# Routing and expert stage of a fused retention and mixture kernel: key digits made together, 16-bit index tables, routing work moved to GpSimd, and new costs in the planner's table

## The chip, the cores and the metric

One core of one Trainium2 chip. The metric is the device time of the whole kernel in microseconds (us), the median of three timed runs. A profiled execution with a trace of every instruction lies beside them. The core's engines are TensorE (PE, with its weight loads as PEld), VectorE (DVE), ScalarE (ACT) and GpSimd (POOL). Each takes its instructions in order, and the queue of SyncE (SP) issues most of the DMAs.

## The reference

```python
# attention (retention) over B=4, H=8, S=768, D=64, then:
x = attn_out as 3072 tokens x 512
h = x @ w_in; g = s * max(h, 0)**2 + b; x = g @ w_out          # 512 -> 2048 -> 512
# second stage: 8 experts, 384 tokens each
logits = x @ w_gate                                            # 3072 x 8
order = np.argsort(-logits.flatten())
for idx in order:                                              # greedy: best pair first
    tok, e = idx // 8, idx % 8
    if assigned[tok] >= 0 or counts[e] >= 384: continue
    assigned[tok] = e; counts[e] += 1
for e in range(8):
    out[assigned == e] = max(x[assigned == e] @ w1[e], 0) @ w2[e]   # 512 -> 1024 -> 512
```

The greedy assignment is sequential by nature. The kernel does it in eight rounds: each round finds the expert that fills up first and the logit at which it does, closes it, and goes on with the tokens that are left.

## The kernel before, in words

The kernel runs four parts one after the other: the retention and first dense stage (`retention`, `moes`), the middle blocks (`moe1`), the last block with the logits (`h_pair`, `x_last`), and the part that the change touches, from line 886 on: the search for each expert's tokens, and the experts' two matrix products.

Matrix products are done in two halves per operand (high part and remainder, `h` and `l`, `gh` and `gl`), as three matmuls each.

**The last part.** For each round i the work is:

- `begin(i)` (L924): over the open experts each token's best logit `m`, the expert `mx` that it belongs to, a one-hot `Eh` (L947) and a sixteenfold copy `EH` of it, in four pieces of 128x768 on ScalarE (L954); then the logit as an integer key (L960, L961) and its first digit (L969, L974, L980).
- `search(i)` (L1002): the threshold is found digit by digit, in six steps. In each the PE counts with 24 matmuls (L988) how many tokens of each expert reach each digit value, DVE picks the largest value at which some expert is full (L1034 to L1040) and compares the next digit with it (L969 for the digit, L1027, L980). At the end come the state updates (L1081 to L1084) and the slot numbers (L1073 to L1092).
- `index(i)` (L1102): from the slots two one-hot tables `oa` and `ob` and a payload `pay` are built on DVE (L1117 to L1126), 24 matmuls (L1131) and one more (L1139, two entries in the trace) put the token numbers in place, and DVE makes `idx` (L1142, L1145), the 384 rows of the round's expert.
- `fetch(i)` (L1149): three indirect DMAs by GpSimd (L1156) gather these rows from `x2d` in DRAM into the tile `big`, 128 rows each. The PE transposes them (L1170, twelve of 128x128 in groups), ACT and DVE split them into `gh` and `gl` (L1164, L1166).
- The expert's products in `mains` (L1333): `eh_unit` (L1295, 96 matmuls of 384 columns an expert) and `ey_unit` (L1315, 72 of 512 columns). Its rows are scattered to the output by GpSimd (L1323).
- Weights: `e_load` by SP (L1259), `e_high` on ACT (L1267), `e_low` on DVE (L1277).

In round 0 the last 128 rows of `x2d` are still being made (`x_last`, L854) while the search runs, and their contribution comes through a one-hot matmul (`one_hot` L1208, `last_row`, L1183). The first gather waits until the row blocks 21 to 23 are written to `x2d` (L861 on ACT, L863 the DMA).

**What sets the order.** Each engine runs its program in order, so the order of the instructions decides who waits. It is made at build time by a small planner (`Plan`, L76). Each strand of work is a generator that yields records `(engine, nanoseconds, needs, gives, latency, keep)`. The planner holds a clock for each engine and the time of each named result, and always emits the record that can begin first. `keep` is added to the needs of a PE record (600 ns for the search and the transposes) so that the PE gets other work in the meantime. What the planner takes as a gather's price is in `fetch`: 1000 ns of GpSimd for each of the three, and 2600 ns from there to the data (`LAT`, L118):

```python
LAT = {"PE": 190.0, "ACT": 50.0, "DVE": 50.0, "POOL": 2600.0, "Q": 2500.0}
yield op("POOL", 1000, ("idx", i), "w3" if i else "x2d", gives=("xg", i, t))
yield pe(340, *(("xg", i, t) for t in range(GT)), need, gives=("T", i, kc), keep=KEEP)
```

A record that is a lambda is a condition in the planner's order, and no instruction.

Of the kernel before, what the change touches and what calls it, by code (L numbers as in the profile page):

```python
# [20 lines left out]
F32 = mybir.dt.float32  # L21
# [11 lines left out]
FAR = 1.0e6  # L33
# [111 lines left out]
def kernel(  # L145
# [653 lines left out]
    POOL.tensor_copy(jt, iota[:, 0:NT + 1, None].to_broadcast([128, NT + 1, 2]))  # L799
    closed = rt.tile([128, E], F32, name="closed")  # L800
# [120 lines left out]
    SH = [32 - sum(BW[:s + 1]) for s in range(len(BW))]  # L921

    def begin(i):
# [32 lines left out]
        plan.add(repeat(), 100)  # L956
        yield dve(720)
# [4 lines left out]
        d = start_of(digit(key, 0))  # L962
        yield dve(950, gives=("cmp", i, 0))
        d, cmp = compare(d, 1, NT)
        ME[i] = (key, mx, EH.rearrange("p c r e -> p c (r e)"), d, cmp)
# [36 lines left out]
    def search(i):  # L1002
# [11 lines left out]
        else:  # L1014


            key, mx, EH, d, cmp = ME.pop(i)
            for s, w in enumerate(BW):

                n = (1 << w) - 1 if s + 1 < len(BW) else NL  # L1020
                yield pe(810 if n == NT else 620, ("cmp", i, s), ("EH", i, NC - 6), gives=("cnt", i, s), keep=KEEP)
                cnt = count(EH, cmp, n)
                yield dve(360)
# [70 lines left out]
        if not last:  # L1094
            yield dve(400)
            ta = rt.tile([128, NC], F32, name="ta")
            DVE.scalar_tensor_tensor(ta, s1[:, NC:], float(CAP), stb[:, NC:2 * NC], op0=OP.is_le, op1=OP.mult)
            DVE.tensor_tensor(Uf, Uf, ta, op=OP.subtract)
            if i + 2 < E:
                yield from begin(i + 1)  # L1100

    def index(i):  # L1102

        yield dve(630, ("s1", i))
        s1 = SLOT.pop(i)
        sl = rt.tile([128, NC], I32, name="sl")
        DVE.scalar_tensor_tensor(sl, s1[:, 0:NC], -1.0, s1[:, NC:], op0=OP.add, op1=OP.add)
# [4 lines left out]
        lowp = rt.tile([128, NC], I32, name="lowp")  # L1112
        DVE.tensor_scalar(lowp, sl, UP - 1, None, op0=OP.bitwise_and)
        DVE.tensor_scalar(sl, sl, UP.bit_length() - 1, None, op0=OP.arith_shift_right)
        yield dve(760)
        ob = rt.tile([128, NC, WP], F16, name="ob")
        DVE.tensor_tensor(ob, sl[:, :, None].to_broadcast([128, NC, WP]),  # L1117
                          iota[:, None, 0:WP].to_broadcast([128, NC, WP]), op=OP.is_equal)
        yield dve(560)
        oa = rt.tile([128, NC, UP], F16, name="oa")  # L1120
        DVE.tensor_tensor(oa, lowp[:, :, None].to_broadcast([128, NC, UP]),
                          iota[:, None, 0:UP].to_broadcast([128, NC, UP]), op=OP.is_equal)
        yield dve(880, gives=("pay", i))
        pay = rt.tile([128, NC, 2, UP], F16, name="pay")
        DVE.tensor_scalar(pay[:, :, 1, :], oa, pcv[:, 1, 0:1], None, op0=OP.mult)
        DVE.tensor_tensor(pay[:, :, 0, :], oa, pcv[:, 0, :, None].to_broadcast([128, NC, UP]), op=OP.mult)  # L1126
# [21 lines left out]
    def fetch(i):  # L1148
# [50 lines left out]
    def one_hot():  # L1199

        yield dve(600, "sl0", ("x", NF2 - 1, 3, None), gives="oneh")
# [5 lines left out]
        for k in range(GT):  # L1207
            DVE.tensor_scalar(o[:, k * 128:(k + 1) * 128].rearrange("p (u v) -> p u v", u=UP), at, float(k * 128), SL0,  # L1208
# [199 lines left out]
    plan.add(e_low(), 200)  # L1408
# [87 lines left out]
```

## Time and profile before

| | |
|---|---|
| median of 3 timed runs | 1021.79 us (1015.84 to 1022.62) |
| the profiled execution, its own time | 1010.83 us |
| its span, first to last instruction | 1009.0 us |
| mean granted TensorE clock | 0.992 |
| PE busy | 971.9 us (96%) |
| DVE, ACT, POOL busy | 708.6, 472.0, 68.9 us |

How to read it: PE is busy nearly all the time, so shares of the whole span show little. A row of the timeline gives the time for which its engine stood still before it in brackets, with what ended it. The rows of a timeline merge equal instructions that follow each other ("x24"), with the time from the first start to the last end. Ends of matmuls are modelled, so the distance from one matmul's start to the next one's is its price when the PE is not waiting.

### The profile page before, as it was taken

The numbers are of one execution on the slowest core, as the hardware profiler recorded it, in microseconds if no ns is written. First come the engines' busy times: TensorE is split into PE (matmuls) and PEld (weight loads), VectorE is DVE, ScalarE is ACT, GpSimd is POOL, SyncE is SP. The second block draws the span as 40 slices with busy tenths as digits, with TensorE's granted clock in tenths as the row PEclk, the third lists the DMA queues.
The fourth block names the chain that finished last, engine by engine and source line by source line (L and its number), as shares of the span: only waits on it lengthen the run. The fifth ranks groups of instructions, "written<-read, shape, count | busy, mean of one in ns | idle before, by whom it ended". The sixth has DMA issues, their size and how long they took to land.

```text
span 1009.0 us, 18595 instructions
## 1 busy us (share of the span) xinstructions
PE 971.9 (96%) x7296; PEld 854.8 (85%) x7296; DVE 708.6 (70%) x1778; ACT 472.0 (47%) x953; POOL 68.9 (7%) x90
## 2 busy tenths in 40 slices
PE   7899999999999999999999999989999998999897
PEld 6899998889998999989989777777878787788796
DVE  5898983688887788788772623677878777788510
ACT  6766766444344444444443552343453543345411
POOL 2000000000000000000000100011120311113111
PEclk8999999999999999999999999999999999999999
DMA  9233442532212021212130100334243433427400
GB/s 344 88 129 139 151 146 95 160 99 83 89 32 91 26 70 57 64 63 64 53 110 14 47 1 2 115 127 157 85 176 128 147 117 114 157 85 243 175 32 32
DMA packets 32952, 103.58 MB, mean 103 GB/s; under 512 B 4512, under 2 KB 4896, under 8 KB 32864
## 3 DMA queue, kind: packets, MB, share of 16 engines
q1 hardware_dynamic: 28080, 88.15, 26.5%
q0 software_dynamic: 3920, 12.89, 3.6%
q10 hardware_dynamic: 864, 1.35, 0.4%
q8 instruction: 57, 0.93, 0.4%
q14 instruction: 31, 0.25, 0.1%
HBM read 89.53 MB, written 12.85 MB: 101 GB/s over the span
## 4 chain that ended last, share of the span: by engine, by line
PE 86%; DMA 6%; issue 4%; POOL 2%; DVE 1%; ACT 0%; POOLq 0%; SPq 0%; ACTq 0%; DVEq 0%
PE b L434 27%; PE b L467 22%; PE b L1295 10%; PE b L1315 9%; DMA big<-x2d,idx 4%; PE b L854 4%; PE b L341 3%; PE b L354 3%; PE b L988 2%; PE b L368 2%; POOL big L1156 1%; PE b L1170 1%; PE b L362 1%; PE b L837 1%; DMA x2d<-tmp 1%
## 5 line engine op out<-in xcount | busy, mean ns | idle before, releaser
L490 DVE SCALAR_TENSOR_TENSOR scr<-tmp,wg 128x512 bf16<-128x512 f32 x288 | 198.2, 688 | 9.0 <-ACT tmp L477 3.7
L434 PE MATMUL b<-xh,h 128*128 128x256 f32 (+1 forms) x640 | 189.0, 295 | 1.5 <-ACT xh L659 1.5
L434 PE MATMUL b<-xl,h 128*128 128x256 f32 (+1 forms) x640 | 188.2, 294 | 0.3 <-DVE xl L661 0.3
L434 PE MATMUL b<-xh,l 128*128 128x256 f32 (+1 forms) x640 | 188.2, 294 | 0.0
L434 PEld LDWEIGHTS b<-xh,h 128*128 128x128 f32 x640 | 122.3, 191 | 11.0 <-ACT xh L659 1.7
L434 PEld LDWEIGHTS b<-xl,h 128*128 128x128 f32 x640 | 122.3, 191 | 7.9 <-DVE xl L661 0.5
L467 PE MATMUL b<-h,rh 128*128 128x512 f32 x320 | 128.7, 402 | 0.0
L467 PE MATMUL b<-l,rh 128*128 128x512 f32 x320 | 126.1, 394 | 0.0
L467 PE MATMUL b<-h,rl 128*128 128x512 f32 x320 | 124.8, 390 | 0.0
L434 PEld LDWEIGHTS b<-xh,l 128*128 128x128 f32 x640 | 122.2, 191 | 2.8
L441 ACT ACTIVATE r<-b 128x256 f32<-128x256 f32 x112 | 43.0, 384 | 166.1 <-PE b L434 158.7
L1295 PE MATMUL b<-gh,h 128*128 128x384 f32 x256 | 89.6, 350 | 0.0
L1300 ACT ACTIVATE hh<-b 128x384 fp32r<-128x384 f32 x64 | 31.4, 491 | 123.5 <-PE b L1295 122.8
L1295 PE MATMUL b<-gl,h 128*128 128x384 f32 x256 | 86.2, 337 | 0.2 <-DVE gl L1166 0.2
L1295 PE MATMUL b<-gh,l 128*128 128x384 f32 x256 | 86.3, 337 | 0.0
L1267 ACT ACTIVATE h<-eraw 128x1024 fp32r<-128x1024 f32 x64 | 66.8, 1056 | 27.1 <-DMA eraw<-in_w_dram 26.5
L1277 DVE TENSOR_TENSOR l<-eraw,h 128x1024 fp32r<-128x1024 f32 x64 | 77.5, 1216 | 2.4 <-ACT h L1267 2.3
L1315 PE MATMUL b<-h,hh 128*128 128x512 f32 x192 | 78.3, 408 | 0.0
L1315 PE MATMUL b<-h,hl 128*128 128x512 f32 x192 | 75.7, 394 | 0.0
L1315 PE MATMUL b<-l,hh 128*128 128x512 f32 x192 | 75.6, 394 | 0.0
L1303 DVE SCALAR_TENSOR_TENSOR hl<-b,hh 128x384 fp32r<-128x384 f32 x64 | 35.5, 554 | 53.9 <-ACT hh L1300 53.3
L467 PEld LDWEIGHTS b<-h,rl 128*128 128x128 f32 x320 | 60.1, 188 | 13.7
(250 smaller groups left out, 1794.4 us busy)
## 6 DMA issues: line engine op xcount, KB each, us to landing
eraw<-in_w_dram SPq DMA_DIRECT2D x64, 512.0 KB, 4.2
q<-in_qkv_dram SPq DMA_DIRECT2D x36, 512.0 KB, 5.2
raw<-in_w_dram SPq DMA_DIRECT2D x32, 512.0 KB, 4.6
x2d<-tmp SPq DMA_DIRECT2D x21, 256.0 KB, 7.0
qdec<-in_dec_dram SPq DMA_DIRECT2D x18, 256.0 KB, 2.8
wg<-in_wgT_dram SPq DMA_DIRECT2D x4, 512.0 KB
x2d<-tmp ACTq DMA_DIRECT2D x3, 256.0 KB
first1h<-in_qkv_dram SPq DMA_DIRECT2D x1, 512.0 KB
```

The costliest lines, as they stand in the source:

```text
L341: PE.matmul(ps[s][:, p * 128:(p + 1) * 128], kT[ss, p, :], qT[ss, p, :], start=(p == 0), stop=True, skip_group_check=True)
L434: PE.matmul(ph, a[:, ks], b[..., kc, :], start=(kc == 0 and n == 0), stop=(kc == KC - 1 and n == 2))
L441: ACT.activation(r, ph, AF.Relu)
L467: PE.matmul(X2[blk][t], a[:, ts], b, start=(f == 0 and i == 0), stop=(f == NF - 1 and i == 2))
L490: DVE.scalar_tensor_tensor(scr, x, 1.0, WG[e], op0=OP.mult, op1=OP.mult, accum_out=of[:, e:e + 1])
L854: PE.matmul(XB[c][:, ns], a[:, cs], b[:, ns], start=(f == 0 and i == 0), stop=(f == NF - 1 and i == 2), skip_group_check=True)
L1267: ACT.activation(hi, ERAW[n], AF.Copy)
L1277: DVE.tensor_tensor(lo, ERAW.pop(n), hi.bitcast(F32), op=OP.subtract)
L1295: PE.matmul(ph, a[:, ks], b[:, kc, :], start=(kc == 0 and n == 0), stop=(kc == KC - 1 and n == 2))
L1300: ACT.activation(hh, ph, AF.Relu)
L1303: DVE.scalar_tensor_tensor(hl, ph, 0.0, hh.bitcast(F32), op0=OP.max, op1=OP.subtract)
L1315: PE.matmul(Y[i, t], a[:, ts], b, start=(f == 0 and j == 0), stop=(f == NF2 - 1 and j == 2))
```

## The change

Six things, all in the last part:

- `begin` makes all later digits of the key at once, in two DVE instructions over 128x5x24 with a table `shifts`, where each search step made its own digit.
- One of the four pieces of `EH` is copied by GpSimd in place of ACT.
- The four state updates after a round's search (`s8`, `rem`, `Uf`, `closed`) become six GpSimd instructions; DVE's next instruction on `Uf` waits for them.
- `index` builds its tables in bf16 from bf16 inputs, in pairs of columns, and half of the payload is made by ACT.
- `one_hot` moves from DVE to GpSimd.
- The planner's table: a gather is now priced at 1250, 1250 and 1700 ns on GpSimd and 3700 ns to the data; round 0's count matmuls get 250 ns of `keep` in place of 600; three strands get other priorities, and the rest of the numbers follow the edits.

```diff
+    pc2 = rt.tile([128, NC], BF, name="pc2")
+    POOL.tensor_copy(pc2, pcv[:, 0, :])
...
+    shifts = rt.tile([128, 2, len(BW)], I32, name="shifts")
+    for s in range(1, len(BW)):
+        POOL.memset(shifts[:, 0, s:s + 1], SH[s])
+        POOL.memset(shifts[:, 1, s:s + 1], (1 << BW[s]) - 1)
...
         def repeat():
-            for c in range(0, NC, 6):
+            for c in range(0, NC - 6, 6):
                 yield act(830, ("Eh", i), gives=("EH", i, c))
...
+        def repeat_last():
+            c = NC - 6
+            yield op("POOL", 1200, ("Eh", i), gives=("EH", i, c), lat=60)
+            POOL.tensor_copy(EH[:, c:c + 6], Eh[:, c:c + 6, None, :].to_broadcast([128, 6, 128 // E, E]))
...
+        yield dve(500)
+        DVE.tensor_tensor(dgs[:, 1:], of[0], of[1], op=OP.arith_shift_right)
+        DVE.tensor_tensor(dgs[:, 1:], dgs[:, 1:], of[2], op=OP.bitwise_and)
...
-                yield pe(810 if n == NT else 620, ("cmp", i, s), ("EH", i, NC - 6), gives=("cnt", i, s), keep=KEEP)
+                yield pe(810 if n == NT else 620, ("cmp", i, s), ("EH", i, NC - 12), ("EH", i, NC - 6), gives=("cnt", i, s), keep=KEEP if i else 250.)
...
-                    DVE.scalar_tensor_tensor(b, d, up, digit(key, s + 1), op0=OP.mult, op1=OP.add)
+                    DVE.scalar_tensor_tensor(b, d, up, dgs[:, s + 1], op0=OP.mult, op1=OP.add)
...
-            yield dve(900)
-            s8 = rt.tile([128, 1], F32, name="s8")
-            DVE.tensor_scalar(s8, w8c, sm, FAR, op0=OP.is_equal, op1=OP.mult)
-            DVE.scalar_tensor_tensor(rem, rem, ca, s8, op0=OP.subtract, op1=OP.add)
-            DVE.tensor_tensor(Uf, Uf, ug, op=OP.subtract)
-            DVE.scalar_tensor_tensor(closed, w8, sm, closed, op0=OP.is_equal, op1=OP.add)
+            yield op("POOL", 1100, ("ca", i), gives=("upd", i), lat=60)
+            s8 = rt.tile([128, 1 + E], F32, name="s8")
+            POOL.tensor_scalar(s8[:, 0:1], w8c, sm, FAR, op0=OP.is_equal, op1=OP.mult)
+            POOL.tensor_scalar(s8[:, 1:], w8, sm, None, op0=OP.is_equal)
+            POOL.tensor_tensor(s8[:, 0:1], s8[:, 0:1], ca, op=OP.subtract)
+            POOL.tensor_tensor(rem, rem, s8[:, 0:1], op=OP.add)
+            POOL.tensor_tensor(closed, closed, s8[:, 1:], op=OP.add)
+            POOL.tensor_tensor(Uf, Uf, ug, op=OP.subtract)
...
-            yield dve(400)
+            yield dve(400, ("upd", i))
             ta = rt.tile([128, NC], F32, name="ta")
...
+        def which(a, n):
+            t = rt.tile([128, NC // 2, n, 2], BF, name="o" + "ab"[a])
+            DVE.tensor_tensor(t, slh[:, a].rearrange("p (a b) -> p a b", b=2)[:, :, None, :].to_broadcast(t.shape),
+                              jt[:, None, 0:n, :].to_broadcast(t.shape), op=OP.is_equal)
+            return t
...
+        def tokens():
+            yield act(420, ("oa", i), gives=("pay1", i))
+            ACT.activation(pay[:, :, 1], oa, AF.Copy, scale=pcv[:, 1, 0:1])
...
-            yield op("POOL", 1000, ("idx", i), "w3" if i else "x2d", gives=("xg", i, t))
+            yield op("POOL", 1250 if t + 1 < GT else 1700, ("idx", i), "w3" if i else "x2d", gives=("xg", i, t), lat=3700)
...
-        yield dve(600, "sl0", ("x", NF2 - 1, 3, None), gives="oneh")
+        yield op("POOL", 900, "sl0", ("x", NF2 - 1, 3, None), gives="oneh", lat=60)
...
-            DVE.tensor_scalar(o[:, k * 128:(k + 1) * 128].rearrange("p (u v) -> p u v", u=UP), at, float(k * 128), SL0,
+            POOL.tensor_scalar(o[:, k * 128:(k + 1) * 128].rearrange("p (u v) -> p u v", u=UP), at, float(k * 128), SL0,
...
-    plan.add(one_hot(), -300)
+    plan.add(one_hot(), 1500)
...
-    plan.add(e_low(), 200)
+    plan.add(e_low(), 400)
```

What the new table does to the order, at three places. In the changed kernel the lines are L1006 (count, before L988), L1171 (the small matmul that precedes `idx`, before L1139), L1202 (transposes, before L1170), L1327 and L1347 (the expert products, before L1295 and L1315), L960 and L965 (the pieces of `EH` on ACT and GpSimd, before L954), L1188 (gather, before L1156) and L863 (row copy, before L861).

First the PE, up to the transposes of round 2's rows (`big`). Before:

```order
L988 MATMUL b_8608<-cmp,EH 128x63
L1315 MATMUL b_8279<-h_8061,hh 128x512
L1315 MATMUL b_8279<-l_8250,hh 128x512
L1315 MATMUL b_8279<-h_8061,hl 128x512
L1315 MATMUL b_8285<-h_8061,hh 128x512
L1315 MATMUL b_8285<-l_8250,hh 128x512
L1315 MATMUL b_8285<-h_8061,hl 128x512
L1170 MATMUL b_8656<-ident,big 128x128 x3
L1170 MATMUL b_8663<-ident,big 128x128 x3
```

And in the changed kernel:

```order
L1006 MATMUL b_8588<-cmp,EH 128x63
L1327 MATMUL b_8576<-gh,h_8075 128x384
L1327 MATMUL b_8576<-gl,h_8075 128x384
L1327 MATMUL b_8576<-gh,l_8334 128x384
L1347 MATMUL b_8373<-h_7904,hh 128x512
L1347 MATMUL b_8373<-l_8218,hh 128x512
L1347 MATMUL b_8373<-h_7904,hl 128x512
L1202 MATMUL b_8640<-ident,big 128x128 x3
L1202 MATMUL b_8645<-ident,big 128x128 x3
```

The count at the top of the first piece is the first of the next round's six, that of the second piece is the second of them. Between L1139 of round 2 and these transposes the program of before has 24 count matmuls, 18 of L1295 and 15 of L1315; the changed one has, between L1171 and L1202, 48, 24 and 18. Rounds 1 and 3 read alike. In round 4 the numbers are 24, 24 and 18 (before 24, 18, 15), in round 5 48, 27 and 18 (before the same 24, 18, 15), in round 6 no count, 45 and 9 (before 18 and 18), and in round 7 no count, 84 and 57 (before 30 and 9).

Second GpSimd, around the gather of round 1. Before:

```order
L1156 DMA big<-x2d,idx 128x512 x6
L1322 MEMSET spacer 1x1
L1323 DMA out_dram<-yo,idx 3072x512
L1322 MEMSET spacer 1x1
L1323 DMA out_dram<-yo,idx 3072x512
```

And now:

```order
L1188 DMA big<-x2d,idx 128x512 x3
L1240 TENSOR_SCALAR oneh<-c_6310,sl_6726 128x128 x3
L1099 TENSOR_SCALAR s_7736<-c_6310,sm 128x1
L1100 TENSOR_SCALAR s_7736<-c_6310,sm 128x8
L1101 TENSOR_TENSOR s_7736<-s_7736,ca 128x1
L1102 TENSOR_TENSOR rem<-rem,s_7736 128x1
L1103 TENSOR_TENSOR closed<-closed,s_7736 128x8
L1104 TENSOR_TENSOR Uf<-Uf,ug 128x24
L965 COPY EH<-Eh 128x768
L1188 DMA big<-x2d,idx 128x512 x3
L1354 MEMSET spacer 1x1
L1355 DMA out_dram<-yo,idx 3072x512
```

In the queue that held gathers and scatters alone stand now a round's updates and the copy of the next round's `EH` piece, ahead of the gather.

Third ACT, where the last full row block (`x2d`) that the first gather needs is copied out. Before:

```order
L861 ACTIVATE tmp<-b_6680,sb 128x512
L863 DMA x2d<-tmp 128x512
L1267 ACTIVATE h_7179<-eraw 128x1024
L1267 ACTIVATE h_7213<-eraw 128x1024
L1135 ACTIVATE ixs<-b_7188 32x24
L1267 ACTIVATE h_7230<-eraw 128x1024
L954 ACTIVATE EH<-Eh 128x768 x4
```

And now:

```order
L1167 ACTIVATE ixs<-b_7171 32x24
L960 ACTIVATE EH<-Eh 128x768 x2
L863 ACTIVATE tmp<-b_6682,sb 128x512
L865 DMA x2d<-tmp 128x512
L960 ACTIVATE EH<-Eh 128x768
L1299 ACTIVATE h_7257<-eraw 128x1024
```

Two pieces of round 1's `EH` stand now ahead of the row's copy, and the weights' high parts behind it. From that row's last product to the first transposes of round 0 the PE has now 15 more matmuls of 256 columns (33 after 18), one more count of 63 columns and one of 31 more, and not the 25 of the index, which stand earlier.

## Rows read from the trace of the kernel before

**Rows 1.** The page, part 1: busy us (share of span) xinstructions.

```profile
PE 971.9 (96%) x7296; PEld 854.8 (85%) x7296; DVE 708.6 (70%) x1778; ACT 472.0 (47%) x953; POOL 68.9 (7%) x90
```

**Rows 2.** Waits of PE, 650 to 950 us: us in total, times, longest.

```profile
PE b L1170 <- DMA big<-x2d,idx: 18.3, 10, 3.4
PE b L854 <- DVE u L1218: 0.7, 1, 0.7
```

**Rows 3.** Timeline of PE, round 2: start, us, instruction [idle before].

```profile
738.19 0.33 PE L1295 MATMUL b<-gh,h 128*128 128x384 f32 x1
738.37 0.33 PE L1295 MATMUL b<-gl,h 128*128 128x384 f32 x1
738.81 0.40 PE L1139 MATMUL b<-ixs,c 32*128 32x24 f32 x2
...
746.49 0.39 PE L1315 MATMUL b<-h,hl 128*128 128x512 f32 x1
746.72 0.38 PE L1170 MATMUL b<-ident,big 128*128 128x128 f32 x2
749.42 0.55 PE L1170 MATMUL b<-ident,big 128*128 128x128 f32 x3 [2.32 <-DMA big<-x2d,idx]
```

**Rows 4.** Timeline of PE: other waiting transposes, rounds 0, 1, 3, 4, 5.

```profile
659.33 0.44 PE L1170 MATMUL b<-ident,big 128*128 128x128 f32 x2 [1.51 <-DMA big<-x2d,idx]
...
662.33 0.33 PE L1170 MATMUL b<-ident,big 128*128 128x128 f32 x1 [1.64 <-DMA big<-x2d,idx]
...
705.96 0.33 PE L1170 MATMUL b<-ident,big 128*128 128x128 f32 x1 [1.78 <-DMA big<-x2d,idx]
...
792.97 0.33 PE L1170 MATMUL b<-ident,big 128*128 128x128 f32 x1 [2.41 <-DMA big<-x2d,idx]
...
837.49 0.48 PE L1170 MATMUL b<-ident,big 128*128 128x128 f32 x1 [3.37 <-DMA big<-x2d,idx]
...
882.51 0.44 PE L1170 MATMUL b<-ident,big 128*128 128x128 f32 x2 [2.29 <-DMA big<-x2d,idx]
```

**Rows 5.** Timeline of PE around a count, round 2.

```profile
701.58 0.94 PE L988 MATMUL b<-cmp,EH 128*128 128x63 bf16 x24
702.35 0.48 PE L1315 MATMUL b<-h,hh 128*128 128x512 f32 x1
```

**Rows 6.** Timeline of DVE and POOL about the gather of round 2.

```profile
738.47 0.36 DVE L947 TENSOR_TENSOR Eh<-c,mx 128x192 bf16<-128x192 f32 x1
...
739.51 0.18 DVE L1145 TENSOR_REDUCE idx<-rm 128x3 int32<-128x24 f32 x1
...
741.84 2.34 DVE L1277 TENSOR_TENSOR l<-eraw,h 128x1024 fp32r<-128x1024 f32 x2
...
740.47 0.99 POOL L1156 DMA_INDIRECT big<-x2d,idx  x1 [25.28 <-PE b L1295]
```

**Rows 7.** Timeline of ACT: the four pieces of EH in round 1.

```profile
653.13 3.02 ACT L954 ACTIVATE EH<-Eh 128x768 bf16<-128x768 bf16 x4
```

**Rows 8.** The window behind the longest wait (busy us, PEclk), PE in it.

```profile
838.00:842.00 4.00, 4.00 (x40) 3.35 (x38) 3.01 (x8) 3.11 (x5) 0.00 (x0) 0.72 0.00 0
...
839.25 0.63 PE L1315 MATMUL b<-h,hl 128*128 128x512 f32 x1
```

**Rows 9.** Timelines of POOL and DVE early in the kernel: GpSimd's prices.

```profile
9.90 1.49 POOL L627 TENSOR_TENSOR qdec0l<-qdec0h,vc 128x512 f32<-128x512 f32 x1
11.35 1.04 POOL L627 TENSOR_TENSOR qdec1h<-qdec0h,vc 128x512 f32<-128x512 f32 x1
...
9.76 0.73 DVE L236 TENSOR_TENSOR first1h<-first1h,qdec0l 128x512 f32<-128x512 f32 x1
...
555.75 0.31 POOL L799 CAST jt<-c 128x128 bf16<-128x128 f32 x1
...
556.29 0.52 POOL L816 MEMSET tmp<- 128x512 f32 x1
556.77 0.48 POOL L888 CAST idx<-c 128x1 int32<-128x1 f32 x1
```

More of the change, by code (lines that the diff above doesn't have):

```diff
@@ L951, in repeat @@
         def repeat():
-            for c in range(0, NC, 6):
+            for c in range(0, NC - 6, 6):
                 yield act(830, ("Eh", i), gives=("EH", i, c))
                 ACT.activation(EH[:, c:c + 6], Eh[:, c:c + 6, None, :].to_broadcast([128, 6, 128 // E, E]), AF.Copy)
+        def repeat_last():
+            c = NC - 6
+            yield op("POOL", 1200, ("Eh", i), gives=("EH", i, c), lat=60)
+            POOL.tensor_copy(EH[:, c:c + 6], Eh[:, c:c + 6, None, :].to_broadcast([128, 6, 128 // E, E]))
         plan.add(repeat(), 100)
+        plan.add(repeat_last(), 0)
         yield dve(720)
@@ L962, in begin @@
         d = start_of(digit(key, 0))
+        dgs = rt.tile([128, len(BW), NC], I32, name="dgs")
+        of = [key[:, None, :].to_broadcast([128, len(BW) - 1, NC])]
+        of += [shifts[:, k, 1:, None].to_broadcast([128, len(BW) - 1, NC]) for k in range(2)]
         yield dve(950, gives=("cmp", i, 0))
         d, cmp = compare(d, 1, NT)
-        ME[i] = (key, mx, EH.rearrange("p c r e -> p c (r e)"), d, cmp)
+        yield dve(500)
+        DVE.tensor_tensor(dgs[:, 1:], of[0], of[1], op=OP.arith_shift_right)
+        DVE.tensor_tensor(dgs[:, 1:], dgs[:, 1:], of[2], op=OP.bitwise_and)
+        ME[i] = (dgs, mx, EH.rearrange("p c r e -> p c (r e)"), d, cmp)
     def digit(key, s):
@@ L1014, in search @@
         else:
-            key, mx, EH, d, cmp = ME.pop(i)
+            dgs, mx, EH, d, cmp = ME.pop(i)
             for s, w in enumerate(BW):
                 n = (1 << w) - 1 if s + 1 < len(BW) else NL
-                yield pe(810 if n == NT else 620, ("cmp", i, s), ("EH", i, NC - 6), gives=("cnt", i, s), keep=KEEP)
+                yield pe(810 if n == NT else 620, ("cmp", i, s), ("EH", i, NC - 12), ("EH", i, NC - 6), gives=("cnt", i, s), keep=KEEP if i else 250.)
                 cnt = count(EH, cmp, n)
-                yield dve(360)
+                yield dve(180)
                 b = rt.tile([128, NC], F32, name="b")
@@ L1102, in index @@
     def index(i):
-        yield dve(630, ("s1", i))
+        yield dve(800, ("s1", i))
         s1 = SLOT.pop(i)
-        sl = rt.tile([128, NC], I32, name="sl")
-        DVE.scalar_tensor_tensor(sl, s1[:, 0:NC], -1.0, s1[:, NC:], op0=OP.add, op1=OP.add)
+        sl = rt.tile([128, 2, NC], I32, name="sl")
+        DVE.scalar_tensor_tensor(sl[:, 1], s1[:, 0:NC], -1.0, s1[:, NC:], op0=OP.add, op1=OP.add)
         if i == 0:
@@ L1111, in index @@
             plan.T["sl0"] = plan.clk["DVE"]
[L1112 to L1126, printed above, removed]
+        DVE.tensor_scalar(sl[:, 0], sl[:, 1], UP - 1, None, op0=OP.bitwise_and)
@@ new lines, in index @@
+        DVE.tensor_scalar(sl[:, 1], sl[:, 1], UP.bit_length() - 1, None, op0=OP.arith_shift_right)
+        slh = rt.tile([128, 2, NC], BF, name="slh")
+        DVE.tensor_copy(slh, sl)
+        def which(a, n):
[3 more added lines that the diff above has]
+            return t
@@ new lines, in index @@
+        yield dve(370)
+        oa = which(0, UP)
+        pay = rt.tile([128, NC // 2, 2, UP, 2], BF, name="pay")
+        plan.T["oa", i] = plan.clk["DVE"] + LAT["DVE"]
+        def tokens():
+            yield act(420, ("oa", i), gives=("pay1", i))
+            ACT.activation(pay[:, :, 1], oa, AF.Copy, scale=pcv[:, 1, 0:1])
+        plan.add(tokens(), -100)
+        yield dve(470)
+        ob = which(1, WP)
+        yield dve(370, gives=("pay", i))
+        DVE.tensor_tensor(pay[:, :, 0], oa, pc2.rearrange("p (a b) -> p a b", b=2)[:, :, None, :].to_broadcast(oa.shape),
+                          op=OP.mult)
@@ L1127, in index @@
         yield lambda: not i or i - 1 in XDONE
-        yield pe(640, ("pay", i), *((("gl", i - 1, KC - 1),) if i else ()), gives=("ix", i), keep=KEEP)
+        yield pe(640, ("pay", i), ("pay1", i), *((("gl", i - 1, KC - 1),) if i else ()), gives=("ix", i), keep=KEEP)
         ix = bank(7)
         for c in range(NC):
-            PE.matmul(ix[0:2 * UP, 0:WP], pay[:, c].rearrange("p a g -> p (a g)"), ob[:, c, :],
+            PE.matmul(ix[0:2 * UP, 0:WP], pay[:, c // 2, :, :, c % 2].rearrange("p a g -> p (a g)"),
+                      ob[:, c // 2, :, c % 2],
@@ L1400 @@
     plan.add(searches(), 0)
-    plan.add(first_index(), -500)
+    plan.add(first_index(), -200)
     plan.add(indexes(), -100)
-    plan.add(one_hot(), -300)
+    plan.add(one_hot(), 1500)
     plan.add(row_out(), 200)
```

## The prediction, made before the changed kernel ran

> **What bounds the kernel now.** I read the page first, then the waits of the PE in the part that the change touches, then the timeline at each of those waits. The page has the PE busy for 971.9 of 1009.0 us [rows 1]; DVE, which loses most instructions here, is busy for 708.6. The waits from 650 to 950 us have nearly one line only: the transposes of the gathered rows wait for the gather, 18.3 us in ten waits, the longest 3.4. All that the PE waits for DVE in a row of its own is 0.7 us [rows 2]. So instructions taken from DVE or ACT are worth nothing by themselves; what counts is how much of the 18.3 us goes.
>
> The timeline of round 2 shows how such a wait arises [rows 3]. The small matmul L1139, from which DVE makes the row numbers, starts at 738.81. The first two transposes run at 746.72, since their rows are there, and the third stands 2.32 us until 749.42. The third block of rows thus comes 10.6 us after L1139, and the order had put some 8.1 us of work in between. DVE ends `idx` at 739.51 + 0.18 = 739.69 and GpSimd starts the first gather at 740.47 [rows 6]. From there to the data it is 8.95 us; the planner's table had 3 x 1.0 + 2.6, and 0.6 of `keep`, which is 6.2 us. The transposes are not urgent, but the PE works in order, so their wait is a wait of everything. Rounds 1, 3, 4 and 5 lose 1.78, 2.41, 3.37 and 2.29 us in the same way, round 0 loses 1.51 + 1.64 [rows 4]. What is left of the 18.3 us, 18.3 - 1.78 - 2.32 - 2.41 - 3.37 - 2.29 - 3.15 = 3.0 us, is round 7's; round 6 had none.
>
> **The change part by part: the gather's price.** The table now has 1.25 + 1.25 + 1.7 + 3.7 + 0.6 = 8.5 us, and the order shows what came of it. A matmul of 384 columns costs 0.18 us and one of 512 columns 0.23 (start to start [rows 3]), 24 counts 0.77 us [rows 5]. In rounds 1 to 3 the order puts 24 counts, 6 matmuls of 384 and 3 of 512 columns more between L1171 and the transposes: 0.77 + 1.08 + 0.69 = 2.5 us. In round 4 it is 6 and 3 without the counts, 1.8 us; in round 5 24 counts, 9 and 3, 3.1 us; in round 7 54 and 48, over 20 us. Against the waits: 1.78, 2.32 and 2.41 go (each under 2.5), of 3.37 goes 1.8 and 1.6 stays, 2.29 goes, round 7's 3.0 go. Together 13.6 us. The slack that remains is small in rounds 2 and 3: 0.2 and 0.1 us.
>
> Round 0 is bound by the last row block: ACT copies it out, it goes to DRAM, then the gather may start. The order puts 15 matmuls of 256 columns (half of 0.23 each, 1.7 us) and two more counts (at most 0.77 each) in front of the transposes, and takes away the 25 small ones of the index (about one count's worth): some 2.4 us more cover for waits of 3.15 us in all. But two pieces of `EH` now precede the row's copy on ACT, 3.02 / 4 = 0.75 us each [rows 7]. They can start when `Eh` is made, which in round 2 is as L1139 starts (738.47 + 0.36 [rows 6] against 738.81 [rows 3]), and three matmuls of 512 columns after that the row is ready: 1.5 - 0.7 = 0.8 us late. So 2.4 - 0.8 = 1.6 us are gained; the bounds are 0 and 3.15.
>
> **The clock.** Behind the longest wait, 3.37 us in round 4, the granted clock of the window 838 to 842 us is 0.72, its mean over the two levels of 2.4 and 1.2 GHz, and a matmul that lasts 0.39 us elsewhere lasts 0.63 [rows 8, 3]. That costs (1 - 0.72) x 4 = 1.1 us. After 2.41 us of idling (round 3) no such stretch follows. With 1.6 us left in round 4 I count the 1.1 us as gained.
>
> **What GpSimd takes over.** Ahead of each gather stands now the copy of a 128x768 piece. No row shows this copy. From below: a memset of 128x512 took 0.52 us, times 1.5 is 0.8. From above: a cast of 128x128 took 0.31 us, times 6 is 1.9 [rows 9]. Nearest in size is the two-input product of 128x512, 1.04 us; I take 1.4. `Eh` ends at 738.83 and the gather began at 740.47, so 1.64 us hide the copy; at 1.9 each gather is 0.3 late, which rounds 2 to 4 can't absorb. I charge 0.3 us in all (bounds 0 and 1).
>
> GpSimd's instructions also meet DVE's. The third product of 9.90 us took 1.49 us while DVE ran a product of two SBUF operands at 9.76 for 0.73 us; the one at 11.35 took 1.04 [rows 9]. The Trainium skill has a rule for this (SBUF — State Buffer, "Who interferes with whom"): a DVE instruction with two SBUF inputs and a GpSimd instruction that reads SBUF exclude each other for the whole of the instruction. By that rule the product that met DVE's waits, and the trace agrees with 1.49 - 1.04 = 0.45 us; applied to every gather and copy it gives the first rival's time below, and without it the sum stands.
>
> The six updates cost from 6 x 0.1 to 6 x 0.48 us (the cast of one column [rows 9]), and up to two remainders L1277 of 1.17 us each [rows 6] may run first: 0.6 to 5.2 us. DVE needs them only at `ta`; between lie in the order two such remainders, the slots and the index tables, about 5 us. So nothing is charged, with 0.2 us a round as upper bound.
>
> The first count of a round needs ACT's three pieces (2.3 us), GpSimd's one and DVE's first comparison. In round 1, where ACT also copies the row, cover is short: I charge 0.3 us. The rest, the digits together, bf16 tables and half of the payload on ACT, shortens DVE's chain by some 2 us a round, which the PE does not wait for: 0. `one_hot` on GpSimd runs behind the gather of round 0 and has several us until its matmul: 0.
>
> **Sum.** 13.6 + 1.6 + 1.1 - 0.3 - 0.3 = 15.7 us. Against the profiled execution of 1010.8 us (span 1009.0 and 1.8 around it) this gives 995.1 us. The median of the timed runs is 1021.8, 11 us above that execution; what those runs lose in addition is not in the trace, so I leave it: 1021.8 - 15.7 = 1006 us.
>
> **Rivals.** First, the gathers slip with their cover: GpSimd is held up by DVE before and in the gather. For it speak the 1.49 against 1.04 us, and that `cmp` and L1277 run just then; against it, that gathers beside L1277 were mostly near 1 us before (740.47: 0.99). By the mechanism an L1277 of 1.17 us ahead of the copy or the gather costs about 1.2 us in each of seven rounds, 8 us: 1014 us.
>
> Second, slower than before: the updates sit in GpSimd's queue behind scatters, which wait for the experts' output rows, and behind DVE's two-input instructions. DVE then stands at `ta`, and with it the next round's first comparison, the counts, and the PE. It decides from the point where the updates come later than 5 us after `ca`. To undo the gain it takes 15.7 / 7 = 2.2 us a round; with 3.5 us in each of seven rounds the time is 1006 + 24 = 1030 us. For it speaks that GpSimd's queue is in order and nearly full of waits; against it, that the planner prices the queue too and puts most updates ahead of the scatters of the same time.
>
> Third, more is gained: if the 11 us between the timed runs and the profiled one are the same waits, longer and with the halved clock behind them more often, half of them go too: about 1000 us or less, and 997 with round 0 and 4 fully covered.
>
> **How the numbers follow.** I give the forecast 0.60 (its own range 1001 to 1011), the first rival 0.17, the second 0.08, the third 0.15. A measurement of this kernel can tell about 1% from no change, which puts the bounds at 1011.6 and 1032. Faster by over 1%: 0.57 of the forecast, 0.15, and 0.02 of the first rival, 0.74. Within 1%: 0.03, 0.15, and 0.03 of the second, 0.21. Slower: 0.05. The range that leaves out 2 in 10 takes in the third case down to 995 and the first up to 1017.
>
> **What would show it.** Right: the waits of the PE for `big` fall from 18.3 to some 4 us, most of it in rounds 0 and 4, and no window behind round 4 shows a clock under 1. The distance from L1171 to the third block's data stays 10.1 to 11.7 us. Wrong: if that distance grows by 1 us and more, with the GpSimd copy or a long indirect DMA before it, the first rival holds; if new lines appear in which counts wait for DVE, and DVE's `ta` for GpSimd, the second. If the waits go and the span falls by less than 12 us, the work itself has become dearer, which no step here allows.

## The result, and the profile after

The changed kernel takes 991.46 us (median of 6 runs, 991.1 to 992.7). Six runs of the kernel before beside them had a median of 1015.87 us. The ratio is 0.974, 95% interval 0.971 to 0.978. Ratios here are worked out from means and leave out slow runs, those over 1.5% above the fastest of their batch (two of the kernel before, at 1026.7 and 1027.0 us). The forecast was 1006 us with 995 as the lower end of its range: the time lies 3.5 us below that end, and the gain of 24.4 us is 8.7 more than the 15.7 of the forecast. The other 5.9 us between 1006.1 and 991.5 are the base, which was 1021.8 us when the forecast was made. The profiled executions stand at 1010.83 and 991.12 us, their spans 20.0 us apart.

The page of the changed kernel, part 1 (the counterpart of [rows 1]):

```profile
PE 968.6 (98%) x7297; PEld 852.8 (86%) x7297; DVE 696.3 (70%) x1726; ACT 471.0 (48%) x954; POOL 92.8 (9%) x153
```

The PE does the same work in a shorter span. DVE lost 12 us and POOL gained 24. The waits of the PE from 650 to 950 us, the view of [rows 2]:

```profile
PE b L1202 <- DMA big<-x2d,idx: 1.7, 2, 1.0
PE b L1171 <- ACT ixs L1167: 0.7, 1, 0.7
PE b L856 <- DVE u L1250: 0.5, 1, 0.5
PE b L1006 <- DVE cmp L998: 0.3, 1, 0.3
```

The first row was 18.3 us in ten waits. The PE's timeline shows round 2 without a wait, and then the two that are left, in the rounds 4 and 5:

```profile
720.99 0.40 PE L1171 MATMUL b<-ixs,c 32*128 32x24 f32 x2
...
731.57 0.60 PE L1202 MATMUL b<-ident,big 128*128 128x128 f32 x4
...
809.11 0.66 PE L1202 MATMUL b<-ident,big 128*128 128x128 f32 x4 [0.72 <-DMA big<-x2d,idx]
...
851.62 0.66 PE L1202 MATMUL b<-ident,big 128*128 128x128 f32 x4 [0.96 <-DMA big<-x2d,idx]
```

In round 2 the transposes of all three blocks now start 10.6 us after L1171 and find their rows there; before, two started at 7.9 us and the third waited until 10.6 [rows 3]. All waits of this view together fell from 19.4 us (18.3, 0.7, and two of 0.2 for `ixs` and `gl`) to 3.2 us, which is 16.2 of the 20.0. The slow clock behind the longest wait is gone: over the windows of 4 us from 600 to 980 us the kernel before lost (1 - clock) x 4 us = 1.7 us in sum, the changed one nothing. Another 0.8 us is chance at the start of the kernel, where the order is the same: the second stage begins at 180.56 us here and at 181.33 there, and at 180.55 in another execution of the kernel before (b_again). Some 1.3 us are not traced to a row.

### The profile page after: what moved, and what is told of

It reads as the page before. It is cut to its first block, busy times and chain, and to the rows that moved or that the text cites. A ratio compares the mean times of both kernels' runs of the same rounds, so it can differ in the third digit from the quotient of the medians.

```text
span 989.0 us, 18653 instructions
## 1 busy us (share of the span) xinstructions
PE 968.6 (98%) x7297; PEld 852.8 (86%) x7297; DVE 696.3 (70%) x1726; ACT 471.0 (48%) x954; POOL 92.8 (9%) x153
## 4 chain that ended last, share of the span: by engine, by line
PE 87%; issue 4%; DMA 4%; DVE 2%; POOL 1%; ACT 1%; SPq 0%; POOLq 0%; ACTq 0%; DVEq 0%
PE b L434 27%; PE b L467 23%; PE b L1347 10%; PE b L1327 9%; PE b L856 5%; PE b L341 3%; PE b L354 3%; PE b L1006 2%; PE b L368 2%; DMA eraw<-in_w_dram 2%; DMA big<-x2d,idx 1%; PE b L1202 1%; PE b L362 1%; PE b L839 1%; POOL out_dram L1355 1%
## 5 line engine op out<-in xcount | busy, mean ns | idle before, releaser
L1327 PE MATMUL b<-gh,h 128*128 128x384 f32 x256 | 89.8, 351 | 0.0
L1327 PE MATMUL b<-gh,l 128*128 128x384 f32 x256 | 86.2, 337 | 0.0
L1327 PE MATMUL b<-gl,h 128*128 128x384 f32 x256 | 86.0, 336 | 0.0
L1309 DVE TENSOR_TENSOR l<-eraw,h 128x1024 fp32r<-128x1024 f32 x64 | 77.3, 1219 | 8.7 <-ACT h L1299 8.7
L1347 PE MATMUL b<-h,hh 128*128 128x512 f32 x192 | 78.0, 406 | 0.0
L1347 PE MATMUL b<-h,hl 128*128 128x512 f32 x192 | 75.6, 394 | 0.0
L1347 PE MATMUL b<-l,hh 128*128 128x512 f32 x192 | 75.4, 393 | 0.0
```

The lines of the kernel that those rows point to most:

```text
L1309: DVE.tensor_tensor(lo, ERAW.pop(n), hi.bitcast(F32), op=OP.subtract)
L1327: PE.matmul(ph, a[:, ks], b[:, kc, :], start=(kc == 0 and n == 0), stop=(kc == KC - 1 and n == 2))
L1347: PE.matmul(Y[i, t], a[:, ts], b, start=(f == 0 and j == 0), stop=(f == NF2 - 1 and j == 2))
```

## The experiments

Fourteen kernels ran. Each ratio is against runs of the kernel before on the same chip; it can differ a little from the quotient of the medians.

| kernel | median us (range) | ratio, 95% interval |
|---|---|---|
| b_again: before, unchanged | 1018.65 (1011.2 to 1026.7) | 1.000 [0.997, 1.004] |
| b_price: before with the new price | 999.17 (995.5 to 1001.7) | 0.982 [0.978, 0.985] |
| b_plan: and 250 ns of keep in round 0 | 997.60 (996.7 to 1003.9) | 0.980 [0.974, 0.986] |
| b_lat6000: before, price to the data 6000 | 994.45 (992.9 to 998.1) | 0.977 [0.973, 0.982] |
| b_plan7000: 7000, and 250 ns of keep | 990.80 (989.4 to 994.1) | 0.974 [0.970, 0.979] |
| b_halfw: b_price, half the weight bytes | 989.59 (989.1 to 990.4) | 0.972 [0.968, 0.976] |
| a_again: changed, unchanged | 992.41 (990.4 to 998.2) | 0.976 [0.972, 0.980] |
| a_oldprice: changed with the old price | 1002.69 (999.6 to 1004.7) | 0.985 [0.981, 0.988] |
| a_lat4700: changed, 4700 | 990.36 (990.0 to 991.0) | 0.973 [0.970, 0.977] |
| a_lat6000: changed, 6000 | 990.93 (990.6 to 992.4) | 0.974 [0.970, 0.978] |
| a_keep600: changed, keep 600 in round 0 | 994.07 (991.4 to 997.8) | 0.976 [0.970, 0.982] |
| a_eh_act: changed, EH on ACT alone | 994.00 (991.9 to 995.2) | 0.974 [0.969, 0.979] |
| a_upd_dve: changed, updates on DVE | 993.14 (992.0 to 994.7) | 0.974 [0.968, 0.979] |
| a_pad: changed, updates 4 us later | 1004.12 (1000.2 to 1005.9) | 0.986 [0.983, 0.990] |

### What the timed runs of before lose beside the profile

b_again has no edit.

> The kernel before, unchanged. Its profile read 1010.8 us, five of its six timed runs so far about 1015.5 and one 1022.6. Theory A (the timed runs lose in the same waits as the profile, and now and then in a halved clock behind one): a profile of 1010 to 1016 us with 17 to 21 us of PE waits for the gathered rows, and a granted clock below 0.99 wherever the time is over 1015. Rival: the 5 us between profile and timed runs have nothing to do with the waits, and are seen at the same clock and the same sum of waits.

The profiled execution took 1019.5 us here, 8.7 us more than the one that I had read, and its trace shows where. PE waits for the rows, then windows of 4 us (the column after the engines is PEclk):

```profile
707.75 0.33 PE L1170 MATMUL b<-ident,big 128*128 128x128 f32 x1 [1.94 <-DMA big<-x2d,idx]
752.86 0.33 PE L1170 MATMUL b<-ident,big 128*128 128x128 f32 x1 [2.41 <-DMA big<-x2d,idx]
798.43 0.33 PE L1170 MATMUL b<-ident,big 128*128 128x128 f32 x1 [2.84 <-DMA big<-x2d,idx]
843.22 1.11 PE L1170 MATMUL b<-ident,big 128*128 128x128 f32 x4 [3.61 <-DMA big<-x2d,idx]
889.47 0.34 PE L1170 MATMUL b<-ident,big 128*128 128x128 f32 x1 [2.64 <-DMA big<-x2d,idx]
```

```profile
708.00:712.00 4.00, 4.00 (x36) 3.19 (x35) 2.61 (x6) 2.94 (x4) 0.00 (x0) 0.59 0.02 5
752.00:756.00 4.00, 3.14 (x10) 2.37 (x10) 2.12 (x5) 2.77 (x4) 0.00 (x0) 0.64 0.03 13
840.00:844.00 4.00, 0.78 (x5) 0.78 (x5) 0.21 (x1) 0.27 (x1) 0.00 (x0) 0.73 0.23 87
844.00:848.00 4.00, 4.00 (x32) 3.09 (x31) 2.64 (x5) 2.79 (x4) 0.00 (x0) 0.50 0.00 0
888.00:892.00 4.00, 2.53 (x9) 2.14 (x10) 1.48 (x5) 2.10 (x4) 0.00 (x0) 0.71 0.10 40
```

Almost the same waits for the rows (19.6 us against 18.3) are followed here by a stretch at the lower clock level, 1.2 GHz, five times (four of them in the rows; the first, behind round 0's waits, has a clock of 0.57 in the window 664 to 668), where the trace of [rows 8] had it once. Summed over the windows from 600 us on it costs 10.3 us against 1.7, and this difference of 8.6 us is about as large as the whole one of 8.7. The account does not close to the tenth: all waits of the PE together are 2.4 us longer here, and the start is 0.8 us shorter. Theory A's mechanism holds, while its range for the profile (1010 to 1016 us) was missed for just this reason, and its bound of 0.99 was a little low, since one run at 0.991 took 1017 us. Over 56 runs of this kernel, in b_again and beside the experiments, the time goes with the mean granted clock: 14 runs below 0.982 had a mean of 1022.0 us, 13 runs at 0.988 and more 1014.9. Their median is 1017.5 us.

> The changed kernel, unchanged. If its gain is that waits and the halved clock behind them are gone, its runs lie close together: 991 to 993 us with a granted clock of 0.993 to 0.995 in each, where those of the kernel before spread over 1011 to 1022 us with clocks of 0.980 to 0.992. Rival: the spread belongs to the chip and not to the kernel, and the changed kernel spreads as far.

The spread is smaller, 990.4 to 998.2 against 1013.2 to 1025.2 us, but not gone: the run at 998.2 has a clock of 0.987, the one at 995.0 of 0.992. The profiled one shows one wait for rows, 1.1 us. So the first statement holds for the median and falls for single runs; what lowered the clock in the run of 998.2 us no trace shows.

### The price alone, and everything but the price

```diff
-            yield op("POOL", 1000, ("idx", i), "w3" if i else "x2d", gives=("xg", i, t))
+            yield op("POOL", 1250 if t + 1 < GT else 1700, ("idx", i), "w3" if i else "x2d", gives=("xg", i, t), lat=3700)
```

> The kernel before with the gather's new price alone (1250, 1250 and 1700 ns of GpSimd and 3700 ns to the data). Theory A (the price earns nearly all that the waits cost; the moves to GpSimd earn nothing by themselves): the waits for the gathered rows fall from 18 to 2 to 6 us, and the time from 1015.9 to 998 to 1002 us. Rival B (relief of DVE and ACT by GpSimd and the bf16 tables earn most): the time stays at 1010 us or above, or the waits appear as new ones of the counts for cmp or EH. Theory C (round 0's gain needs the earlier weight loads): the two waits of round 0, 1.51 and 1.64 us, stay here in whole or in half.

> The changed kernel with the gather's old price (1000 ns each and 2600 ns to the data). Theory A: the waits return in rounds 1 to 6, whose transposes now stand after 7.3 to 8.8 us of PE work behind the row numbers' matmul where the rows come 10 to 11 us after it: 8 to 14 us of waits, and a time of 1002 to 1008 us. Rival B: no more than 3 us are lost, time under 995 us.

Waits of the PE from 650 to 950 us, first in b_price, then in a_oldprice:

```profile
PE b L1170 <- DMA big<-x2d,idx: 6.0, 5, 2.1
PE b L1139 <- ACT ixs L1135: 1.4, 1, 1.4
```

```profile
PE b L1202 <- DMA big<-x2d,idx: 9.0, 10, 2.4
PE b L856 <- ACT u L1248: 0.6, 1, 0.6
```

Both medians fall where theory A put them, yet A's statement that the price earns nearly all is too strong: by these two the price is worth 1015.9 - 999.2 = 16.7 us on the kernel before and 1002.7 - 991.5 = 11.2 on the rest of the change, and the rest 13.2 us without the price and 7.7 with it. In a_oldprice the waits of the rounds 0 and 7 (3.15 and 3.0 us before) are gone, and 12.2 us of the others became 9.0. Theory C falls: round 0's waits for the rows went in b_price too, with one of 1.4 us for `ixs` in their place.

### More price

> The changed kernel with 4700 ns in place of 3700 ns to the data. If the two waits that are left (0.94 us in round 4, 1.18 in round 5) are only a matter of the distance, both go, since the order now has 11.1 to 11.5 us of work there: 989 to 990.5 us against 991.5. Rival: the PE runs out of other work in the same place, so the wait turns up at another line (counts for cmp, ey for hh), and the time is the same or up to 2 us longer.

> The changed kernel with 6000 ns in place of 3700 ns to the data (4700 ns gave 990.36 us and no wait for the rows). The order has 11.5 to 14.5 us of work between the row numbers' matmul and the transposes. Theory A: past the 12.5 us that the rows need at most nothing more is to be had, and the time is that of 4700 ns, 990 to 991 us. Rival: more distance starves the products of the next unit, since the rows come later into gh and gl: new waits for gl or hl and 992 us or more.

With 4700 ns no wait for the rows is left in the changed kernel:

```profile
PE b L856 <- DVE u L1250: 0.5, 1, 0.5
PE b L1202 <- DVE gl L1198: 0.2, 1, 0.2
```

Both came out as theory A said. By its median the kernel with 4700 ns is the fastest here that loads all of the weights, about 1 us below the changed one, with a range that touches its best runs (990.4 us in a_again); 6000 ns brings nothing more.

### The parts one at a time

```diff
-gives=("cnt", i, s), keep=KEEP if i else 250.)
+gives=("cnt", i, s), keep=KEEP)
...
-            for c in range(0, NC - 6, 6):
+            for c in range(0, NC, 6):
-        plan.add(repeat_last(), 0)
```

These are a_keep600 and a_eh_act; a_upd_dve puts back the four DVE lines that the change's diff takes out.

> The changed kernel with 600 ns of keep for round 0's counts again, as before. Theory A (round 0's waits went because the first search ends some 5 us earlier, so the first expert's weights are loaded before the last row block is written, and the gather starts 3.0 us after that row's DMA is issued instead of 6.6): the matmul before idx in round 0 falls back to about 652 us, the row's write and the weights' loads run side by side again, the gather starts 5 to 7 us after the row's issue, and the transposes of round 0, with 7.7 us of work ahead of them in place of 12.1, wait 2 to 4 us: 993.5 to 995.5 us. Rival (the gain is in the cover alone, more counts and row products ahead of the transposes): the gather still starts about 3 us after the row's issue, and the wait is below 1.5 us: 991 to 993 us.

> The changed kernel with the fourth piece of EH on ACT again. My charge for GpSimd's copy was 0.3 us, and it took 0.87 us on the mean there: theory A expects no gain and no loss above 1.5 us from the way back, since the gathers then start up to 0.9 us earlier and the counts up to 0.75 us later: 990.5 to 993 us, with waits of the counts for EH of at most 1 us. Rival (the copy on GpSimd earns its place): counts wait for ACT in most rounds, 995 us or more.

> The changed kernel with the four state updates on DVE again. Theory A: DVE has time to spare between ca and ta, so nothing is lost but some 1 us a round of cover in the order: 990.5 to 993.5 us. Second rival of the prediction turned round (updates on GpSimd come late and hold DVE at ta): the time falls below 990 us and the search's steps run closer together. Third possibility (the relief of DVE is what the move earns): 995 us or more, with waits of counts for cmp.

Theory A's charges were about right. a_eh_act lost 2.5 us by the medians, 1 us above theory A's bound, and its trace shows waits for rows (3.9 us) and none for `EH`, so the rival falls as well; why the rows come later there stays open. a_upd_dve is 1.7 us above the changed kernel, without a new wait for `cmp`. For a_keep600 the way to the gather was as foretold and the wait was not: its gather starts 6.1 us after the row's issue, but round 0 has no wait for rows, since the three indirect DMAs then ran in 1.09 + 0.96 + 0.95 us. Its profiled execution took 991.7 us; the median of 994.1 lies in theory A's range by two runs of 996.5 and 997.8 us at clocks of 0.991 and 0.989, which no trace explains, so it does not bear A out.

### What starts the first gather, and when

The timelines of SP, ACT and POOL in round 0, before and then after:

```profile
644.54 13.22 SPq L1259 DMA_DIRECT2D eraw<-in_w_dram  x6
...
648.41 0.33 ACTq L863 DMA_DIRECT2D x2d<-tmp  x1
...
654.97 1.01 POOL L1156 DMA_INDIRECT big<-x2d,idx  x1 [96.26 <-DMA x2d<-tmp]
```

```profile
639.48 20.48 SPq L1291 DMA_DIRECT2D eraw<-in_w_dram  x8
...
649.14 0.33 ACTq L865 DMA_DIRECT2D x2d<-tmp  x1
...
652.13 1.40 POOL L1188 DMA_INDIRECT big<-x2d,idx  x1 [4.73 <-DMA x2d<-tmp]
```

Before, the row block was issued 3.9 us after the first four weight blocks of 512 KB began, and the gather followed 6.6 us later; in the changed kernel it was issued 9.7 us after them, and the gather followed 3.0 us later. Where the row came 9.7 us after the weights (a_lat4700, a_oldprice and a_upd_dve too) it is 2.98 to 2.99 us, and 4.5 to 7.7 us where it came 3.9 to 6.9 us after them (b_price, b_plan, b_lat6000, b_plan7000, a_keep600, a_eh_act). The DMA issues of 644 to 664 us (last column: median us from issue to landing) show that it is the row's own write, in b_price, the changed kernel and b_halfw, whose edit comes next and which halves the weights' bytes at the old spacing of 3.9 us:

```profile
eraw<-in_w_dram SPq DMA_DIRECT2D x7, 512.0 KB, 5.4
x2d<-tmp ACTq DMA_DIRECT2D x1, 256.0 KB, 6.5
```

```profile
x2d<-tmp ACTq DMA_DIRECT2D x1, 256.0 KB, 2.0
```

```profile
x2d<-tmp ACTq DMA_DIRECT2D x2, 256.0 KB, 2.3
```

The write beside full-size weights lands after 6.5 us, the one that comes after them after 2.0. In b_halfw the row is the median of two writes, one ahead of the weights; the one beside half of their bytes took 2.4.

### Who makes the rows late in b_price

```diff
-SP.dma_start(t, w12[bass.ds(EREG[i], 1), f].rearrange("o p a n -> p (o a) n"))
+SP.dma_start(t[:, 0:1], w12[bass.ds(EREG[i], 1), f, :, 0:1].rearrange("o p a n -> p (o a) n"))
...
-            ACT.activation(hi, ERAW[n], AF.Copy)
+            ACT.activation(hi, ERAW[n][:, 0:1].to_broadcast([128, 2, 512]), AF.Copy)
```

and the same for `lo` on DVE.

> The kernel before with the new price (b_price) and only the first half of each weight block loaded, used twice: the output leaves out the second halves. Same instructions in the same order, half the bytes of the weights. In b_price the third block of rows came 12.2 to 13.4 us after the row numbers' matmul in rounds 2 to 5, where the kernel before had 10.6 to 11.7, and the DMA engines were full (share 0.8 to 1.06) while they came. Theory (the gathered rows share the DMA engines with the weights, and that sets the distance): it falls to 9.5 to 11 us, the waits of rounds 2 to 5 go but for 0.5 us each, and the time falls from 999 to 992 to 995 us. Rival (the distance is GpSimd's time and a fixed way from there): 12 us as before, and 998 us or more.

Round 2 on the PE and the load of the DMA engines (the last two columns: share of the 16 engines, GB/s), first b_price, then b_halfw:

```profile
734.31 0.40 PE L1139 MATMUL b<-ixs,c 32*128 32x24 f32 x2
...
746.57 0.55 PE L1170 MATMUL b<-ident,big 128*128 128x128 f32 x3 [0.95 <-DMA big<-x2d,idx]
```

```profile
740.00:742.00 2.00, 2.00 (x31) 1.70 (x30) 1.62 (x9) 0.18 (x1) 0.92 (x2) 1.00 1.02 338
744.00:746.00 2.00, 1.62 (x29) 1.12 (x27) 1.00 (x7) 1.59 (x2) 1.08 (x2) 1.00 1.04 365
```

```profile
734.92 0.40 PE L1139 MATMUL b<-ixs,c 32*128 32x24 f32 x2
...
745.80 0.85 PE L1170 MATMUL b<-ident,big 128*128 128x128 f32 x6
```

```profile
740.00:742.00 2.00, 2.00 (x31) 1.64 (x30) 1.73 (x6) 0.49 (x1) 1.52 (x2) 1.00 0.97 298
744.00:746.00 2.00, 2.00 (x32) 1.62 (x31) 1.08 (x3) 1.46 (x2) 0.58 (x1) 1.00 0.09 31
```

The theory holds, and the time is lower than it said. The indirect DMAs take GpSimd as long as in b_price (0.99, 1.30 and 1.95 us in round 2), but the rows are there at 10.9 us after L1139 at the latest, and the engines are nearly idle by 744 us, where b_price fills them until 746 and beyond. No wait for rows is left in any round. So in b_price the PE waits for bytes that the weights hold up. The Trainium skill has the rule (DMA: Bandwidth & Descriptors, "Rules for kernel authors"): transfers issued from two engines share the same 16 DMA engines, with their packets interleaved. The trace agrees on the sharing, by 12.3 against at most 10.9 us; the interleaving no run here shows.

### The second rival, built

```diff
+            pad = rt.tile([128, 512], F32, name="pad")
+            for _ in range(8):
+                POOL.memset(pad, 0.0)
             s8 = rt.tile([128, 1 + E], F32, name="s8")
```

> The changed kernel with eight needless memsets of 128x512 on GpSimd ahead of a round's updates, at 0.52 us each (rows 9) 4.2 us, in the same order of instructions. It puts the second rival's claim to the test. In the changed kernel's trace the updates end 0 to 4.7 us before DVE's ta (4.08, 2.49, 4.70, 0.65, 0, 0.80, 3.64 us in the rounds 0 to 6), so ta is now late in rounds 1, 3, 4, 5 and 6 by 1.7, 3.5, 4.2, 3.4 and 0.5 us, 13 us together. Second rival's price: the PE loses what DVE loses, 1004 us. Theory A: the PE works on the experts' products meanwhile, and only where counts of the next round are due at once does it wait: 993 to 998 us, with waits of counts for cmp or EH.

```profile
PE b L1205 <- DMA big<-x2d,idx: 5.1, 3, 2.0
PE b L1006 <- POOL EH L965: 1.5, 1, 1.5
PE b L1330 <- DVE hl L1338: 1.1, 1, 1.1
PE b L1006 <- DVE cmp L998: 0.8, 2, 0.6
```

The rival's price was met to 0.1 us by the timed median, and theory A's range missed by 6. The way was partly another: DVE stands behind `ta` (in round 3 for 2.9 us, until the last update), which delays `idx` behind it in the same queue, and with it the gather (in round 3 it starts 4.4 us after L1174 and not 1.3 as in the changed kernel), so it is in the main the rows again that the PE waits for, 5.1 us in the rounds 3 to 5.

### Numbers alone

> The kernel before with the gather's price at 1250, 1250 and 1700 ns and 6000 ns to the data, nothing moved. The order has 11.3 to 12.3 us of work between the row numbers' matmul and the transposes of rounds 1 to 7 (b_price 8.9 to 10.3), where the rows came 11 to 13.4 us after it in b_price. Theory (the numbers suffice, the moves earn nothing by themselves): waits for the rows of 0 to 1.5 us a round, 3 us in all, and 993 to 996 us. Rival (the moves earn the rest, since counts are not ready as cover): new waits for cmp, gl or l, and 998 us or more.

> The kernel before with 7000 ns to the data and 250 ns of keep for round 0's counts, nothing moved; 12.5 to 13.4 us of work stand ahead of the transposes in every round. Theory (numbers suffice): no wait for the rows above 0.5 us, and 990 to 993 us, the changed kernel's time. Rival (the moves earn the rest): 996 us or more, with waits for other lines, as the 1.9 us for l in b_plan.

Waits of the PE in b_plan7000, 650 to 950 us:

```profile
PE b L988 <- DVE cmp L980: 0.6, 1, 0.6
PE b L854 <- DVE u L1218: 0.3, 1, 0.3
PE b L1295 <- DVE gl L1166: 0.3, 1, 0.3
```

The theory holds twice. Without one moved instruction, and with DVE as busy as before (709.2 us), the gather's price and one `keep` in the planner's table bring the kernel before to 990.8 us, the changed kernel's time within what can be told. The moves to GpSimd, the digits made together and the 16-bit tables are not needed for it. At the price of 3700 ns they, or the strands' new priorities, earn some 6 us: b_plan, which has the price and the `keep` and nothing else, took 997.6 us (its own forecast was 996 to 999) with 4.8 us of waits for rows. Which of them does it stays open: the priorities were not run alone, and each of the two moves that were taken back cost only 1.7 to 2.5 us, hardly more than the changed kernel's own medians differ (1.0 us).

## Why the prediction was wrong, point by point

**The step that failed** is the last of the sum: "what those runs lose in addition is not in the trace, so I leave it". That left 11.0 us in the forecast, and the changed kernel's median lies 0.3 us above its profiled execution (991.46 and 991.12). So 10.6 of the 14.6 us by which the forecast was too high are this term, and 4.0 are the sum before it. In the 11 us were the same waits, with the lower clock behind more of them: 8.6 us in b_again's trace, the only longer execution that has a trace. A kernel that loses the waits loses most of these stretches too; one run of six in a_again still has a clock of 0.987. This was the third rival, to which I gave 0.15, with 1000 or 997 us. I had the clock row of one wait [rows 8] and took "after 2.41 us of idling no such stretch follows" from it as a rule; b_again has such stretches behind 1.94 and 2.41 us, and none behind 2.84. And part of the 11 us was chance: 1021.8 us was a high draw of three runs, and against the median of 56, 1017.5, the same 15.7 us would have read 1002.

**The gather's price**, 13.6 us: right in its mechanism and, by luck, to the tenth. In the rounds 1 to 7 the waits fell from 18.3 - 3.15 = 15.15 to 1.7 us, by 13.5. Two misses cancel: round 4 kept 0.7 us in place of 1.6, and round 5, where I saw none, 1.0, since the rows came 12.4 us after L1171 and not 10.6 as before. GpSimd in that round, where L1171 stands at 839.22:

```profile
841.41 1.47 POOL L1188 DMA_INDIRECT big<-x2d,idx  x1 [1.28 <-DVE idx L1177]
843.18 1.87 POOL L1188 DMA_INDIRECT big<-x2d,idx  x1 [0.30 <-issue]
```

The gather starts 0.6 us later after that matmul than before, as it waits for DVE's `idx`; its three DMAs end 0.4 us later still (before, the third was the long one, 1.97 us); and from there to the rows it takes 5.3 us in place of 4.5. In round 4 the distance was 10.8 us, as foretold. In the rounds 1, 2, 3 and 6 the PE came 10.5 to 11.1 us after L1171 and did not wait, so there it was no longer than that.

**Round 0**, 1.6 us: mis-sized. All of the 3.15 us went. The row's copy came 0.7 us later by the two traces, near the 0.8, but that is luck. The two pieces of `EH` did not hold it up: ACT was done with them and stood for 0.34 us until the row's product came from the PE.

```profile
648.42 0.69 ACT L863 ACTIVATE tmp<-b,sb 128x512 f32<-128x512 f32 x1 [0.34 <-PE b L856]
```

And my sum held the row's way to the gather fixed. The weights had left the DMA engines by then, because the first search ended some 5 us earlier, and that way shrank from 6.6 to 3.0 us.

**The clock**, 1.1 us: right for the profiled execution (1.7 by the windows), and the wrong size for the timed ones, as above.

**GpSimd's charges**, 0.6 us in all: near. The copy takes 0.87 us on the mean, where I took 1.4; the two waits that came new or longer, for `ixs` and `cmp`, are 0.7 and 0.3 us. The first rival fell as a rule: the gathers of the rounds 1 to 4 start 1.2 to 1.6 us after L1171, not later than before (1.6 to 1.7). Those of the rounds 5 and 6 start after 2.2 and 2.4 us, and round 5 shows the prediction's own sign of this rival, a distance longer by 1.8 us with a long indirect DMA in it; it cost 1.0 us there, and not the 8 of the rival. That DVE holds GpSimd up is true of single instructions, here an update of one column beside the products of L1309:

```profile
675.24 2.34 DVE L1309 TENSOR_TENSOR l<-eraw,h 128x1024 fp32r<-128x1024 f32 x2
...
675.84 1.80 POOL L1101 TENSOR_TENSOR s<-s,ca 128x1 f32<-128x1 f32 x1 [2.12 <-DVE sat L1086]
677.72 0.19 POOL L1102 TENSOR_TENSOR rem<-rem,s 128x1 f32<-128x1 f32 x1
```

It took 1.80 us and ended with them at 677.6; its neighbour of the same shape took 0.19. This is the rule of the Trainium skill that the prediction weighed (SBUF — State Buffer, "Who interferes with whom"), and the trace agrees; the PE did not feel it. The second rival's claim was sound where it was put: the slack is 0 to 4.7 us by rounds and not "about 5", and a_pad shows what lies beyond it. The rival did not come true, because the updates end about 1 us after `ca` when nothing holds them.

Against the profiled execution alone the forecast was 995.1 us and the result 991.1: round 0 gave 1.5 us more, the chance at the start 0.8, the clock 0.6, and some 1.1 us stay without a row.

## What to carry to other kernels

A wait of the engine that bounds the kernel cost its own length here and then, in some executions, a stretch at the lower clock; so before a profiled run is taken for the timed ones, compare their times, and count the difference to the waits if their clocks differ. Where an in-order engine waits for data that nobody needs urgently, give the planner the distance that the trace shows, with a microsecond or two for its spread, before moving any instruction. And ask what else is on the DMA engines when a gather is late: here halving the weights' bytes took every wait for rows away, with GpSimd's part of the gather as long as before.

## What the runs showed of the hardware that was not expected

The length of a wait of the PE does not tell whether the lower clock level follows: in one execution it came behind waits of 1.94, 2.41, 2.64 and 3.61 us and not behind one of 2.84, and behind a wait of 2.41 us it came there and not in the execution read first. What decides, these runs do not show. A write of 256 KB to DRAM landed after 2.0 us with the weights out of the way and after 6.5 us beside them. An indirect DMA of 128 rows held GpSimd for 0.94 to 2.02 us, in no clear relation to the load of the DMA engines: with half the weight bytes the third one of rounds 2 to 5 still took 1.95 us.
